# Sliding-window attention with ALiBi, then a hard-swish MLP, on one core: batches 1 and 2 transposed two pairs at a time, batch 1's diagonal without tables, loads and downs in another order

## The chip, the cores and the metric

The kernel runs on one core of one Trainium2 chip. A core has a matrix engine (TensorE, PE in the profile; its weight loads are shown as PEld), a vector engine (DVE), an activation engine (ACT), a general engine (POOL) and an engine that here only issues transfers (SP). Data lie in on-chip memory (SBUF, 128 partitions), and matmul results in eight banks of PSUM. The metric is the device time of one execution in microseconds (us), less is better. The kernel before takes 338.2 us, the median of three runs from 337.28 to 338.25.

## The reference

Inputs are q, k and v of 8 batches x 8 heads x 576 tokens x 64, in float32, and two weight matrices, 512 x 2048 and 2048 x 512.

```python
scores = scale * np.matmul(q, k.transpose(0, 1, 3, 2))
bias = slopes[:, None, None] * (-np.abs(rel).astype(np.float32))[None, :, :]
mask = (rel >= 0) & (rel < window)                 # rel = query - key, window = 128
scores = np.where(mask, scores + bias[None], -1000000000.0)
attn = softmax(scores);  out = np.matmul(attn, v)  # each head
x = out.transpose(0, 2, 1, 3).reshape(B * S, H * D)  # 4608 tokens x 512
h = x @ w_in
g = h * np.clip(h + 3.0, 0.0, 6.0) / 6.0
return g @ w_out
```

## The kernel before

**Tiling.** Two heads make a pair; pair g is batch g // 4, heads 2(g % 4) and the next. There are 32 pairs. With a window of 128, a block of 128 queries needs its own block of keys (the diagonal scores, `scores_diag`, PSUM tile `scd`) and the block before it (the off scores, `scores_off`, tile `sco`). Keys lie on the partitions and queries along the rows. The exponentials of the scores (`pd`, `po`, and for the short last block `p4buf`) are the weights of the matmuls with v (`av_matmuls`); a column of ones behind v gives the sums. The quotient `avs` is transposed into `xT`, 512 features on the partitions, which the MLP reads. The MLP takes the 4608 tokens in nine chunks of 512: 16 ups for each chunk (`moe_up`: four matmuls of 128x512 into `hps`, ACT's `r`, DVE's product into `gbuf`) and 16 downs (`moe_down`: four matmuls into `ops`; the fourth of each group of four copies `ops` out and stores 128 rows).

**Where bias and mask come from.** For batches 0 and 1 (`tabled`, `full`) a table matmul (`ident` against `tab`, lines 234, 251, 254) puts bias and mask into PSUM ahead of the scores: two of 128x512 for the diagonal of a pair, and for each head one of 128x384 and one of 128x128 for the off blocks. ACT then takes one exponential over both heads of 128x1024 (`exp_full`). For batches 2 to 7 there is no table: ACT adds the bias per partition (`bias_d`, `bias_o`) for each head, and POOL zeroes what the mask forbids (`affine_select`, lines 301, 311, 322).

**How q and k get transposed.** For batches 0 to 2 (`NB_PE`) TensorE transposes them. `load_run` brings one pair's q or k, 128 partitions x 576 float32 (288 KB, lines 91 to 95), `prepare` casts it to bf16 (line 197), and `transposes` makes 36 transposes of 64x64 for a pair (18 of q, 18 of k, line 215) into PSUM, which ACT and DVE copy into `qTb` and `kTb` (line 216). From batch 3 on, `load_tokens` brings tokens, POOL casts them into `tbuf` (line 184), and a transposing DMA from SP's queue (`xbar`, line 189) writes `qTb` and `kTb`. All loads land in four buffers, `ldbuf[0]` to `ldbuf[3]`: q of batches 0 to 2 in the first, k in the second; v0, v2 and k3 in turn in the third; v1 and q3 in the fourth.

**What sets the order.** Each engine works through its instructions in the order in which the program names them (`manual_schedule`); waits come from data and buffers alone. SP's queue is in order too: a load that waits holds what stands behind it. A transfer on the hardware queues also waits for the one eight places before it. `ps_sc` has two PSUM buffers of two banks each, used in turn by `scd`, `sco` and `attend`; `ps_h` has two of one bank for `hps`; `ps_av` and `ps_o` have one each.

**Stages.** `first_batch` does pairs 0 to 3: transposes, scores and exponentials, then values (`attend`) and the transposes into `xT` (`back`). `load_w_in` and `load_w_out` go out on POOL's queue. `second_batch` does pairs 4 to 7: scores, with ups of chunk 0 between them, then `attend` for the four pairs. `fill(n)` emits the next n units of one list of ups and downs; an up is held until `done[0]` says that all tokens of its chunk are in `xT`. `ORDER` gives the list: "U" an up of the new chunk, "D" a down of the chunk before it. `segment` does pairs 8 to 31: in round g the scores of pair g, the exponentials of g, the values of pair g - 1 (`values`, in two halves of three and two query blocks that share the one `av` bank), and `stage_next` for the next batch's casts, transposing DMAs and loads (`LOADS`, `VCAST`: the round in which a load or a cast of v is issued). Batch 1's `pd` and `po` lie in `gbuf[1]`, batch 0's in `w_out_sb`, until chunk 1 and `w_out` take the room.

The gate that starts batch 1's loads is a one-element write of POOL into `ldbuf[0]` (line 523), behind POOL's cast of the last part of v0.

Of the kernel before, what the change touches and what calls it, by code (L numbers as in the profile page):

```python
# [18 lines left out]
def kernel(  # L19
# [9 lines left out]
    nc = tc.nc  # L29
# [12 lines left out]
    NB_PE = 3  # L42
# [53 lines left out]

    def tokens(b, nm):
        if (b, nm) not in ld:
            i = 2 + b % 2 if b < 3 else (3, 2, 0, 1)[(3 * (b - 3) + "qkv".index(nm)) % 4]
            ld[b, nm] = ldbuf[i][:, 0:NQ * H * D].rearrange("p (j h d) -> p j h d", j=NQ, h=H)  # L100
        return ld[b, nm]
# [8 lines left out]
    def constants():  # L110
# [9 lines left out]
        nc.gpsimd.tensor_copy(out=base_b, in_=base_i)  # L120
        nc.gpsimd.affine_select(out=base_b[:, 1, :], in_=base_b[:, 1, :], pattern=[[1, 128]],
# [72 lines left out]
    def prepare(g, copies):  # L194
        for nm, copy in zip("qk", copies):
            pr = prs.tile([128, RT * D], BF16, tag=f"pr{nm}", name="pr")
            copy(out=pr, in_=runs[nm][:, g % NP, :])  # L197
            st[g, nm] = pr

    def transposes(g, copies, nms="qk"):  # L200
        b, hp = divmod(g, NP)
        for nm, dst, copy in (("q", qTb[b % 2], copies[0]), ("k", kTb[b % 2], copies[1])):
            if nm not in nms:
                continue
            src = st.pop((g, nm))
            pool, tag = (ps_h, "h")
            if nm == "k" and g >= NP:
                pool, tag = (ps_av, "av")
            elif NP <= g <= 2 * NP:
                pool, tag = (ps_o, "o")  # L210
            tp = pool.tile([128, RT, RP], BF16, tag=tag, name="tp", padded_shape=[128, 16, 64])
# [6 lines left out]

    def full(g):
        return g < NB_FULL * NP  # L220

    def tabled(g):
        return g < 2 * NP

    def scores_diag(g):
        b, hp = divmod(g, NP)
        qT, kT = qTb[b % 2][:, hp, :, :], kTb[b % 2][:, hp, :, :]
        first = not tabled(g)
        scd = ps_sc.tile([128, 2, 512], FP32, tag="sc", name="scd")
        st[g, "scd"] = scd  # L230
        if tabled(g):
            for e in range(2):
                t = tab[:, 2 * hp + e, 1:2, :]
                nc.tensor.matmul(scd[:, e, :].rearrange("p (j c) -> p j c", j=4), lhsT=ident,
                                 rhs=t.to_broadcast([128, 4, 128]), start=True, stop=False)
# [6 lines left out]
    def scores_off(g):  # L242
        b, hp = divmod(g, NP)
        qT, kT = qTb[b % 2][:, hp, :, :], kTb[b % 2][:, hp, :, :]
        first, foff = not tabled(g), not full(g)
        sco = ps_sc.tile([128, 2, 512], FP32, tag="sc", name="sco")
        if full(g):
# [8 lines left out]
        elif tabled(g):  # L256
            for e in range(2):
                nc.tensor.matmul(sco[:, e, 64:128], lhsT=ident,
                                 rhs=tab[:, 2 * hp + e, 1, 0:64], start=True, stop=False)
        for e in range(2):  # L260
            r = slice(e * D, (e + 1) * D)
            nc.tensor.matmul(sco[:, e, 64:128], lhsT=kT[r, 4, :],
                             rhs=qT[r, 4, 0:LAST], start=first, stop=foff)
# [6 lines left out]
        st[g, "sco"] = sco  # L270
# [13 lines left out]
    def exp_full(g):  # L284
        nc.scalar.activation(out=st[g, "pd"].rearrange("p e j c -> p e (j c)"),
                             in_=st[g, "scd"], func=ACT.Exp, scale=scale)
        nc.scalar.activation(out=st[g, "po"].rearrange("p e j c -> p e (j c)"),
                             in_=st[g, "sco"], func=ACT.Exp, scale=scale)

    def exp_diag(g, e):  # L290
        h = 2 * (g % NP) + e
        pd, sc = st[g, "pd"], st[g, "scd"]
        if tabled(g):
# [11 lines left out]
    def exp_off(g, e):  # L305
# [8 lines left out]
        if tabled(g):  # L314
            if e == 1:
                nc.scalar.activation(out=p4[:, :, 0:64], in_=sc[:, :, 64:128],
                                     func=ACT.Exp, scale=scale)
            return
# [92 lines left out]

    def moe_up(nt, ms):
        gts[nt] = gbuf[nt % 2]
        hps, n = begun.pop((nt, ms), (None, 0))
        if hps is None:
            hps = ps_h.tile([128, NT], FP32, tag="h", name="hps")
# [33 lines left out]
    ORDER = [("UUDDUDUD", "UUDDUDUD", "UUDDUDUD", "UUDDUDUD"),  # L450
# [21 lines left out]
    LOADS = {8: "k3", 9: "v3", 10: "q4", 12: "k4", 13: "v4", 14: "q5", 16: "k5", 17: "v5", 18: "q6",  # L472
             20: "k6", 21: "v6", 22: "q7", 24: "k7", 25: "v7"}

    VCAST = {12: 3, 15: 4, 19: 5, 23: 6, 27: 7}

    def stage_next(g):
        b, hp = divmod(g, NP)
        nb = b + 1
        if g == 2 * NP:  # L480
            cast_tokens(2, "v")
        if nb < B and hp < 2:
# [4 lines left out]
        for n in LOADS.get(g, "").split():  # L487
            load_tokens(int(n[1]), n[0])

    def reload(g):  # L490
        load_run(g, "q", nc.sync)
        load_run(g, "k", nc.sync)

    def first_batch():
        prepare(0, (V, A))
        warm_up(40)
# [7 lines left out]
        prepare(2, (P, P))  # L504
        transposes(2, (V, V))
# [3 lines left out]
        prepare(3, (P, V))  # L509
        transposes(3, (V, V))  # L510
# [12 lines left out]
        nc.gpsimd.memset(runs["q"][:, 0, 0:1], 0.0)  # L523
        for g in range(NP, 2 * NP):
            reload(g)
# [8 lines left out]
        prepare(NP, (P, P))  # L534
        prepare(NP + 1, (P, P))
# [3 lines left out]
        back(3)  # L539
        up_begin(0, 1, 3)  # L540
        done[0] = NP
        fill(2)
        transposes(NP, (V, A))
        biases()
        fill(1)

    def second_batch():
        for g in range(NP, 2 * NP - 1):
            scores(g)
            exp_full(g)  # L550
            fill(1)
            transposes(g + 1, (V, A))
            if g + 2 < 2 * NP:
                prepare(g + 2, (P, P))
            fill(2 if g > NP else 1)
        for j in range(NQ):
            cast_v(1, j, P)
        load_w_out(0)
        for g in range(2 * NP, 3 * NP):
            reload(g)  # L560
        load_tokens(2, "v")
        load_tokens(3, "q")
        load_w_out(1)
        prepare(2 * NP, (P, P))
        for i in range(2, 4):
# [3 lines left out]
        exp_full(g)  # L569
# [114 lines left out]
```

## Time and profile before

| What | Value |
|---|---|
| median of three runs | 338.2 us (337.28, 338.2, 338.25) |
| the profiled execution's own time | 338.87 us |
| its span, first to last instruction | 337.2 us |
| PE busy | 321.7 us (95%) |
| ACT, DVE, POOL busy | 200.2, 166.0, 137.7 us |
| mean granted TensorE clock | 0.995 |
| hardware queue q1 (loads, stores, transposing DMAs) | 41.07 MB |
| software queue q0 (`w_in`, `w_out`) | 4.19 MB |

Busy time adds up the instructions of an engine; matmuls overlap in their pipeline, so their mean duration (359 ns for 128x512) is longer than the pitch at which they follow one another (four in 0.86 us). The share of an engine is a mean over stages. The first scores stand at 7.7 us, the scores of pair 4 at 26.39, of pair 8 at 53.67, of pair 9 at 63.82, of pair 12 at 89.53 and of pair 13 at 97.95. From 319 us on only downs remain. A wait is read as the idle time of an engine just before an instruction and what ended it.

### The profile page before, as it was taken

How to read it: one execution, taken by the hardware profiler on the slowest of the kernel's cores; microseconds unless marked ns; L12 is line 12 of the kernel's file. 1: busy time of each engine (PE TensorE's matmuls, PEld its weight loads, DVE VectorE, ACT ScalarE, POOL GpSimd, SP SyncE). 2: the span in 40 equal slices, each digit the busy share in tenths (PEclk: the TensorE clock that was granted, in tenths of full speed). 3: DMA queues.
4: the chain of work that ended last, by engine and by line, in shares of the span. 5: the costliest groups of instructions: out<-in, count | busy, mean ns of one | idle time of the engine just before them, and what ended most of it. 6: DMA issues, size and time to landing. Idle time of an engine off the chain costs nothing.

```text
span 337.2 us, 7470 instructions
## 1 busy us (share of the span) xinstructions
PE 321.7 (95%) x2963; PEld 170.3 (51%) x2963; DVE 166.0 (49%) x332; ACT 200.2 (59%) x343; POOL 137.7 (41%) x243
## 2 busy tenths in 40 slices
PE   8989998998987999999999999999999999999995
PEld 7564564554443445454567665545554544444442
DVE  4656566454433645464446454554555554434410
ACT  3758875777543675767576757675676344344401
POOL 7524630866546637464746374645333000000000
PEclk9999999999997999999999999999999999999999
DMA  7999999979999899899999998993121100000111
GB/s 279 195 263 278 279 243 205 203 129 192 213 213 177 143 235 177 176 148 241 186 204 132 242 198 175 153 209 89 35 67 49 68 31 31 33 31 31 63 63 62
DMA packets 134771, 51.77 MB, mean 154 GB/s; under 512 B 122832, under 2 KB 127184, under 8 KB 134736
## 3 DMA queue, kind: packets, MB, share of 16 engines
q1 hardware_dynamic: 127200, 41.07, 62.0%
q0 software_dynamic: 4224, 4.19, 7.6%
q10 hardware_dynamic: 3312, 6.03, 5.0%
q8 instruction: 23, 0.38, 0.5%
q14 instruction: 12, 0.10, 0.1%
HBM read 36.70 MB, written 9.44 MB: 137 GB/s over the span
## 4 chain that ended last, share of the span: by engine, by line
PE 78%; ACT 5%; DMA 4%; POOL 4%; DVE 4%; issue 2%; SPq 1%; ACTq 1%; POOLq 0%
PE ops L432 33%; PE hps L403 31%; PE scd L239 3%; ACT r L419 2%; DVE gbuf L420 2%; PE tp L215 2%; DMA ldbuf<-in_k_dram 2%; PE av L343 2%; PE sco L268 2%; DMA ldbuf<-in_q_dram 2%; PE av L335 1%; POOL tbuf L184 1%; PE tb L384 1%; PE w L147 1%; ACT osb L444 1%
## 5 line engine op out<-in xcount | busy, mean ns | idle before, releaser
L420 DVE SCALAR_TENSOR_TENSOR gbuf<-r,hps 128x512 bf16<-128x512 f32 x144 | 98.5, 686 | 120.9 <-ACT r L419 120.8
L403 PE MATMUL hps<-xT,w_in_sb 128*128 128x512 bf16 (+1 forms) x640 | 147.1, 359 | 2.5 <-DVE gbuf L420 1.3
L419 ACT ACTIVATE r<-hps,bias 128x512 f32<-128x512 f32 x144 | 98.8, 689 | 82.5 <-PE hps L403 82.0
L432 PE MATMUL ops<-w_out_sb,gbuf 128*128 128x512 bf16 x576 | 142.9, 380 | 0.8 <-DVE osb L447 0.8
L403 PEld LDWEIGHTS <-w_in_sb 128*128 128x128 bf16 x640 | 59.0, 98 | 57.6 <-issue 5.8
L432 PEld LDWEIGHTS <-gbuf 128*128 128x128 bf16 x576 | 53.6, 98 | 59.4 <-issue 2.2
L301 POOL TENSOR_SCALAR_AFFINE_SELECT pd<-pd 128x512 bf16<-128x512 bf16 x48 | 29.8, 631 | 58.8 <-ACT pd L298 58.7
L311 POOL TENSOR_SCALAR_AFFINE_SELECT po<-po 128x512 bf16<-128x512 bf16 x48 | 30.2, 633 | 30.1 <-ACT po L308 29.5
L184 POOL CAST tbuf<-ldbuf 128x512 bf16<-128x512 f32 (+1 forms) x50 | 29.1, 611 | 14.2 <-DMA ldbuf<-in_k_dram 14.1
L298 ACT ACTIVATE pd<-scd,bias_d 128x512 bf16<-128x512 f32 x48 | 32.0, 688 | 4.4 <-POOL vbuf L177 2.3
L308 ACT ACTIVATE po<-sco,bias_o 128x512 bf16<-128x512 f32 x48 | 33.3, 694 | 0.4 <-ACT osb L444 0.4
L444 ACT COPY osb<-ops 128x512 f32<-128x512 f32 x18 | 10.6, 587 | 29.1 <-PE ops L432 29.1
L354 DVE TENSOR_TENSOR avs<-av,rc 128x384 bf16<-128x384 f32 (+1 forms) x48 | 23.6, 491 | 1.6
L343 PE MATMUL av<-vbuf,pd 128*128 128x65 bf16 x192 | 18.0, 194 | 2.9 <-POOL vbuf L177 2.5
L343 PEld LDWEIGHTS <-pd 128*128 128x128 bf16 x192 | 14.5, 97 | 10.2 <-issue 2.2
L335 PE MATMUL av<-vbuf,po 128*128 128x65 bf16 x192 | 18.3, 193 | 0.7 <-POOL po L311 0.7
L197 POOL CAST pr<-ldbuf 128x576 bf16<-128x576 f32 x20 | 13.0, 667 | 11.7 <-DMA ldbuf<-in_q_dram 9.1
L447 DVE COPY osb<-ops 128x512 f32<-128x512 f32 x17 | 11.7, 687 | 10.5 <-PE ops L432 10.4
L335 PEld LDWEIGHTS <-po 128*128 128x128 bf16 x192 | 14.4, 98 | 4.5 <-POOL po L311 1.0
L319 ACT ACTIVATE p4buf<-sco,bias_d 128x64 bf16<-128x64 f32 x48 | 15.8, 328 | 0.0
L239 PEld LDWEIGHTS <-kTb 64*128 64x128 bf16 x256 | 7.3, 94 | 13.3 <-issue 10.3
L353 DVE RECIPROCAL rc<-av 128x6 f32<-128x6 f32 (+1 forms) x48 | 8.8, 183 | 9.3 <-PE av L343 9.3
(79 smaller groups left out, 226.5 us busy)
## 6 DMA issues: line engine op xcount, KB each, us to landing
ldbuf<-in_v_dram SPq DMA_DIRECT2D x32, 256.0 KB, 5.4
ldbuf<-in_q_dram SPq DMA_DIRECT2D x20, 256.0 KB, 4.9
ldbuf<-in_k_dram SPq DMA_DIRECT2D x20, 256.0 KB, 4.5
out_dram<-osb ACTq DMA_DIRECT2D x18, 256.0 KB, 2.1
out_dram<-osb SPq DMA_DIRECT2D x17, 256.0 KB, 2.7
ldbuf<-in_q_dram SPq DMA_DIRECT2D x12, 288.0 KB, 6.2
ldbuf<-in_k_dram SPq DMA_DIRECT2D x8, 288.0 KB, 7.0
w_in_sb<-in_moe_w_in_dram POOLq DMA_DIRECT2D x4, 512.0 KB, 9.9
```

The source lines that it names most:

```text
L184: nc.gpsimd.tensor_copy(out=tbuf[:m, :, j, :], in_=s[:m, j, :, :].rearrange("p (i e) d -> p i (e d)", e=2))
L298: nc.scalar.activation(out=pd[:, e, :, :].rearrange("p j c -> p (j c)"), in_=sc[:, e, :], func=ACT.Exp, bias=bias_d[:, h:h + 1], scale=scale)
L301: nc.gpsimd.affine_select(out=pd[:, e, :, :], in_=pd[:, e, :, :], pattern=[[0, 4], [1, 128]], channel_multiplier=-1, base=0, compare_op=AL ...
L308: nc.scalar.activation(out=po[:, e, :, :].rearrange("p j c -> p (j c)"), in_=sc[:, e, :], func=ACT.Exp, bias=bias_o[:, h:h + 1], scale=scale)
L311: nc.gpsimd.affine_select(out=po[:, e, :, :], in_=po[:, e, :, :], pattern=[[0, 4], [-1, 128]], channel_multiplier=1, base=-1, compare_op=A ...
L335: nc.tensor.matmul(out_av, lhsT=po[:, e, qt % 4, :], rhs=vb[:, qt - 1, h, :], start=True, stop=False)
L343: nc.tensor.matmul(out_av, lhsT=d, rhs=vb[:, qt, h, :], start=(qt == 0), stop=True)
L354: nc.vector.tensor_tensor(out=st[g, "avs"][:, qts[0]:qts[0] + nq, :, :], in0=av[:, 0:nq, :, 0:D], in1=rc[:, 0:nq, :, :].to_broadcast([128, ...
L403: nc.tensor.matmul(hps[:, lo:hi], lhsT=w_in_sb[:, ks, ts(ms, 128)], rhs=xT[:, ks, ds(src, hi - lo)], start=(ks == 0), stop=(ks == n_ks - 1))
L419: nc.scalar.activation(out=r6, in_=hps, func=ACT.Relu, bias=bias3[:, 0:1], scale=1.0 / 6.0)
L420: nc.vector.scalar_tensor_tensor(out=gts[nt][:, ms, :], in0=r6, scalar=1.0, in1=hps, op0=ALU.min, op1=ALU.mult)
L432: nc.tensor.matmul(ops[nt, sub], lhsT=gts[nt][:, ms, ts(sub, 128)], rhs=w_out_sb[:, ms, :], start=(ms == 0), stop=(ms == n_ms - 1))
```

## The change

- **Loads.** `load_run` for batches 1 and 2 gives way to `load_double`: two pairs (dp 0 or 1) of q or k in two loads of 288 KB, one for the even and one for the odd heads, so that 64 runs of nine tokens of each of two pairs lie on the 128 partitions. The number and size of the loads stay; the order is k, k, q, q for two pairs, where it was q, k for each pair. The one-element write of POOL is to the q buffer still, and the first loads behind it in the program are now k's. Batch 2's loads are named in `first_batch`, behind batch 1's casts; they were named in `second_batch`, behind the casts of v1. v2 and q3 are named behind a new one-element write of POOL into `ldbuf[2]`, which stands after the casts of batch 2's first two pairs.
- **Casts.** `prepare_double`: four casts of 128x576 on POOL for two pairs, as many as before. v1's five casts go from POOL to DVE. The casts of v3 move from `stage_next` of round 12 into round 12 ahead of the values of pair 11.
- **Transposes.** Nine of 128x128 for q or k of two pairs, where there were 36 of 64x64: in batch 1 as one block in a `ps_sc` buffer (`wide_double`, one copy of 128x1152), in batch 2 as five and four in a bank of `av` or `h` (`double`). Batch 0 keeps its 64x64 form.
- **Batch 1's diagonal** has no table (`diag_tabled` holds for batch 0 alone): ACT takes two exponentials with bias, and POOL two selects on `pd`, for each pair. The off blocks keep their tables and one exponential, which now stands behind the next up's `r`.
- **Pair 0's tables** stand among the warm-up matmuls (30, where there were 40); the off tables of pairs 1 and 2 stand ahead of the next pair's transposes. `biases` moves to the start, ahead of the tables on DVE.
- **Ups and downs.** Five ups of chunk 0 use the `av` and `o` banks (`UP_BANKS`). Batch 1's `attend` calls stand among chunk 0's last four ups with one up between them; the scores of pair 8 come after the first two ups of chunk 1. Chunk 1's order in `ORDER` changes. `load_w_out` is named in one row of four. k3 and the other loads in `stage_next` come before the casts and the transposing DMA; k3 moves from `LOADS` of round 8 to the place right behind the casts of v2.

```diff
+    def load_double(b, dp, nm, eng):
+        for e in range(2):
+            eng.dma_start(out=ldbuf["qk".index(nm)][:, ds((2 * dp + e) * RT * D, RT * D)],
+                          in_=src_of[nm][b, ds(4 * dp, 4), :, :].rearrange(
+                              "(i e) (a t) d -> e i a (t d)", e=2, t=RT)[e])
...
+    def prepare_double(b, dp, copies):
+        for nm, copy in zip("kq", copies):
+            pr = prs.tile([128, RT, 2 * D], BF16, tag=f"pr{nm}", name="pr2")
+            for e in range(2):
+                copy(out=pr[:, :, ts(e, D)],
+                     in_=ldbuf["qk".index(nm)][:, ds((2 * dp + e) * RT * D, RT * D)].rearrange(
+                         "p (t d) -> p t d", t=RT))
+            st[b, dp, nm] = pr
...
+    def double(b, dp, nm, part, tag, copy):
+        src = st[b, dp, nm]
+        t0, t1 = ((0, 5), (5, RT))[part]
+        tp = BANKS[tag].tile([128, t1 - t0, 128], BF16, tag=tag, name="tp2",
+                             padded_shape=[128, 8, 128])
+        for t in range(t0, t1):
+            nc.tensor.transpose(tp[:, t - t0, :], src[:, t, :], ident)
...
+    def wide_double(b, dp, nm, copy):
+        src = st[b, dp, nm]
+        wide = ps_sc.tile([128, 2, 512], FP32, tag="sc", name="tp3")
...
+    UP_BANKS = {2: "av", 5: "o", 8: "av", 11: "o", 12: "av"}
...
-    ORDER = [("UUDDUDUD", "UUDDUDUD", "UUDDUDUD", "UUDDUDUD"),
+    ORDER = [("UUDUDUDUD", "UUDUDUDUD", "UUDUDUDD", "UUDDDD"),
...
         if g == 2 * NP:
             cast_tokens(2, "v")
+            load_tokens(3, "k")
+        for n in LOADS.get(g, "").split():
+            load_tokens(int(n[1]), n[0])
         if nb < B and hp < 2:
             cast_tokens(nb, "qk"[hp])
             xbar(nb, "qk"[hp])
         if VCAST.get(g):
             cast_tokens(VCAST[g], "v")
-        for n in LOADS.get(g, "").split():
-            load_tokens(int(n[1]), n[0])
...
         prepare(0, (V, A))
-        warm_up(40)
+        warm_up(20)
+        tables_diag(0)
+        tables_off(0)
+        warm_up(10)
         transposes(0, (V, A))
...
-        nc.gpsimd.memset(runs["q"][:, 0, 0:1], 0.0)
-        for g in range(NP, 2 * NP):
-            reload(g)
+        nc.gpsimd.memset(ldbuf[0][:, 0:1], 0.0)
+        for dp in range(2):
+            for nm in "kq":
+                load_double(1, dp, nm, nc.sync)
         load_tokens(1, "v")
...
         up_begin(0, 0, 3)
         back(3)
+        wide_double(1, 0, "q", V)
+        prepare_double(1, 1, (P, P))
+        for dp in range(2):
+            for nm in "kq":
+                load_double(2, dp, nm, nc.sync)
         up_begin(0, 1, 3)
         done[0] = NP
+        fill(1)
+        wide_double(1, 0, "k", A)
         fill(2)
-        transposes(NP, (V, A))
-        biases()
-        fill(1)
...
             scores(g)
-            exp_full(g)
+            exp_diag(g, 0)
+            exp_diag(g, 1)
             fill(1)
-            transposes(g + 1, (V, A))
-            if g + 2 < 2 * NP:
-                prepare(g + 2, (P, P))
-            fill(2 if g > NP else 1)
+            exp_off_full(g)
+            if g < NP + 2:
+                nm, eng = (("k", V), ("q", V))[g - NP]
+                wide_double(1, 1, nm, eng)
+            fill(2)
         for j in range(NQ):
-            cast_v(1, j, P)
+            cast_v(1, j, V)
...
+        prepare_double(2, 0, (P, P))
+        nc.gpsimd.memset(ldbuf[2][:, 0:1], 0.0)
+        load_tokens(2, "v")
+        load_tokens(3, "q")
+        prepare_double(2, 1, (P, P))
+        fill(1)
+        exp_off_full(g)
         attend(NP)
...
             if g < hi:
                 exp_diag(g, 1)
-            if g + 2 < NB_PE * NP:
-                prepare(g + 2, (P, P))
+            if g == 3 * NP:
+                cast_tokens(3, "v")
             if g > lo:
                 values(g - 1, (0, 1, 2))
```

## The prediction

> **What bounds the kernel now.** The page comes first: busy shares, the granted clock, the chain that ended last.
>
> ```profile
> PE 321.7 (95%) x2963; PEld 170.3 (51%) x2963; DVE 166.0 (49%) x332; ACT 200.2 (59%) x343; POOL 137.7 (41%) x243
> PE 78%; ACT 5%; DMA 4%; POOL 4%; DVE 4%; issue 2%; SPq 1%; ACTq 1%; POOLq 0%
> ```
>
> TensorE is the bound, and a microsecond is won only where TensorE loses an instruction or a wait. The table by stage (stretch, its length, then busy us of PE, PEld, DVE, ACT, POOL, then clock, DMA share, GB/s) says where it idles; I cut where the scores of pair 4, pair 8 with two ups, pair 13 and pair 14 begin or end:
>
> ```profile
> 0.00:26.39 26.39, 22.83 (x420) 16.35 (x421) 15.40 (x36) 14.74 (x19) 13.94 (x32) 1.00 1.05 248
> 26.39:55.85 29.46, 28.02 (x411) 15.52 (x409) 17.90 (x45) 21.90 (x31) 12.46 (x19) 1.00 1.12 253
> 55.85:97.95 42.10, 39.63 (x403) 20.02 (x404) 20.17 (x39) 27.82 (x52) 23.48 (x41) 1.00 1.04 188
> 97.95:110.25 12.30, 9.77 (x69) 4.50 (x69) 4.06 (x9) 6.16 (x11) 9.07 (x17) 0.86 0.95 196
> 110.25:337.20 226.95, 221.47 (x1664) 113.91 (x1663) 108.51 (x205) 129.62 (x231) 78.73 (x137) 1.00 0.60 121
> ```
>
> The last stretch has the same instructions in both kernels: from the scores of pair 13 on the list of ups and downs stands at the same place. Everything is decided before 110. The fourth stretch shows the worst place, a clock of 0.86. The timelines of PE and then POOL show it (start, us, instructions, [idle before, releaser]):
>
> ```profile
> 18.67 0.45 PE L384 MATMUL tb<-ident,avs 128*128 128x128 bf16 x5
> 24.18 0.97 PE L215 MATMUL tp<-ident,pr 64*64 64x64 bf16 x36
> 26.39 0.59 PE L234 MATMUL scd<-tab,ident 128*128 128x512 bf16 x2
> 83.14 0.20 PE L343 MATMUL av<-vbuf,pd 128*128 128x65 bf16 x1 [0.38 <-POOL pd L301]
> 102.33 0.22 PE L343 MATMUL av<-vbuf,pd 128*128 128x65 bf16 x2 [1.92 <-POOL vbuf L177]
> 103.31 0.21 PE L343 MATMUL av<-vbuf,pd 128*128 128x65 bf16 x1 [0.61 <-POOL vbuf L177]
> ```
>
> ```profile
> 22.44 0.66 POOL L197 CAST pr<-ldbuf 128x576 bf16<-128x576 f32 x1 [4.45 <-DMA ldbuf<-in_q_dram]
> 23.95 0.67 POOL L197 CAST pr<-ldbuf 128x576 bf16<-128x576 f32 x1 [0.85 <-DMA ldbuf<-in_k_dram]
> ...
> 98.46 2.83 POOL L184 CAST tbuf<-ldbuf 128x512 bf16<-128x512 f32 x5
> 101.24 2.02 POOL L177 CAST vbuf<-ldbuf 128x1024 bf16<-128x1024 f32 x2
> ```
>
> Batch 3's v is cast behind the five casts of q4, and pair 12's values wait 1.92 and 0.61 us for it. The clock pays too, as the table cut by the microsecond shows (0.50 stands before the DMA share):
>
> ```profile
> 103.00:104.00 1.00, 0.69 (x5) 0.41 (x5) 0.29 (x2) 0.00 (x0) 1.00 (x3) 0.50 1.14 214
> ```
>
> **The change, part by part.** The profiled run took 338.87 us, 1.7 around its span of 337.2; the median of the runs shown is 338.2, 0.7 lower. All sums start at 338.87.
>
> *Head (0 to 22.7).* Tables of pair 0 now stand among the warm-ups, biases before the tables on DVE. 20 warm-ups at 0.11 (40 took 4.45), 2,048 table columns at that pace (1.7) and 10 more end near 6.4 instead of 5.81; pair 0 then sheds its 0.55 of off-diagonal tables. DVE's 16 one-column operations (1.15) sit in its 1.73 idle. I book 0 (-0.5 to +0.6): the next wait covers it.
>
> *Entry into batch 1.* Before, q4 and k4 land at 22.3 and 23.8, are cast by 24.62, and scores of pair 4 start at 26.39. Now four loads (k twice, q twice, 288 KB each) feed the first transposes, and q is asked for first on PE, with all ups behind it. In slots of before the fourth lands at 27.7. But the k loads no longer stand behind the one-element memset on POOL (16.46), so SP issues them at 12.5, right behind v0; the row by microsecond has this queue empty from 14.5 to 19.5. So q takes the first two slots: 22.3 and 23.8 as latest, cast by 24.6. As k already streams when q is issued, the 2.9 us from issue to first byte (16.6 to 19.5) may be hidden; the earliest is about 22.1, cast by 22.9. From the start of q's transposes to the scores of pair 4 it takes: 9 transposes 0.52; three matmuls that begin up 1 and the one that ends up 0, 0.87; ACT's r for up 0, 0.7 with its handing over; then, queued behind it on ACT, the copy of k, 1,152 elements at 0.83 ns each (0.64 for 576 and 0.37 for 256 give that), 1.12 and 0.14 more; 3.35 in all. So these scores start at 28.05 (from 24.65) at the latest, at 26.2 (from 22.9) at the earliest. I take 27.5, nearer to the latest, since the row has the 2.9: **+1.1** (-0.2 to +1.65). w_in's first quarter now shares the engines with k (95 packets per us each, as from 20 to 30, for 195 alone) and lands near 20.8, not 18.0; up 0 asks at 21.3.
>
> *Batch 1 and its values (26.39 to 55.85).* Removed: eight 128x512 tables, 0.53 per pair, and 0.09 less per diagonal, x4 = 2.5. Transposes: four blocks of 36 at 0.70 (pairs 5 to 8) go, 2.8; two nines and two halves of batch 2 come, 36 x 0.058 (0.29 for 5 at 18.67) = 2.1. So work falls 3.2. But waits come: one PSUM pair now turns between scores and transposes. Pair 4: the transposes wait for both diagonal exps (ACT: two r 1.16, two exps 1.16 after the scores: 0.4). Pair 6: its scores wait for DVE's 1,152-element copy (0.75 at 576, so 1.35) behind an up's 0.66: 0.65. Values of pair 4 wait for v1, now five casts of 0.42 on DVE behind the last up's product, where POOL had them ready at 40: 1.2; behind them on DVE stands the product of up 12. Batch 2's halves pass the one "av" bank on, each waiting for the copy of the last (0.6 to 0.75): 1.05 in all.  With 0.1 at pair 5 that is 3.4 of waits where 1.44 was idle: -3.2 + 3.4 - 1.44 = **-1.25** (-3.2 if idle stays 1.44; +0.5 if each wait is 1.5 times as long). ACT does not bind: 3 x 0.58 + 2 x 0.58 + 0.92 = 3.8 per pair under PE's 3.8 to 4.3. On POOL eight selects (0.62) come and v1's five casts go; w_out's four loads, now in a row behind the selects of pair 6, are issued at 40.2 to 43.2 (before 40.0 to 43.4), the last landing by 59.5 for a down near 61.
>
> *Pairs 8 to 10.* Transposes before: 6 x 0.40 = 2.4; now 18 x 0.058 = 1.0. **-1.4** (-1.0 to -1.5). Their casts are on POOL by 50.
>
> [...] The row has 36 at 0.70 and 18 whole ones at 1.04 for two pairs. [...]
>
> *k3 ahead of q3's transposing DMA.* POOL's k3 casts crept from 76.4 to 81.9 behind landings; the selects of pair 10 came late and PE idled 0.38, 0.38 and 0.35 at 82.5. Now k3 goes out when v2 is cast (66), lands by 75, and the casts start when that DMA has read the buffer (75), ending at 78; selects by 80.3, PE asks at 81.2. v3 is issued before k3's transposing DMA, which then starts near 79 (before 81.94, needed 89). **-1.1** (0 to -1.2).
>
> *v3 cast ahead of the values of pair 11.* Needed one pair later; q4's casts stand behind it now. The waits 2.53 go, and the half-clock stretch: four ups' matmuls 1.71 against 0.86, four downs' 1.28 against 0.86, 1.3. **-3.85** (-2.0 to -3.9). Late next: selects of pair 12, whose po exps now follow an osb copy; they end 3.1 us after that down, needed after 4.5.
>
> *Order of ups and downs.* Two more units are spent before pair 12, whose values now have one down, not three, between their halves: **+0.1** (0 to 0.5). The 0.78 wait for the output bank (90) stays, one pair earlier.
>
> Sum: 1.1 - 1.25 - 1.4 - 1.1 - 3.85 + 0.1 = -6.4, **332.5 us**. I do not subtract the 0.7 by which the profiled run stands above the median.
>
> The clock, in this case's row: granted 0.50 from 102.7 to 106.1 after gaps of 1.92 and 0.61. The new wait before q's transposes is 0.2 to 1.9 us long; a like drop there costs at most the same 1.3. [...]
>
> **The rivals.**
> 1. Half clock at the entry (q late, gap near 1.9): 332.5 + 1.3 = 333.8. For: the row above. Against: gaps of 0.73 and 0.26 at 51 left the clock at 1.00.
> 2. Batch 1 gives nothing: its removed work turns into waits (+0.5 in place of -1.25): 334.2. For: three engines pass one PSUM pair round. Against: ACT 21.9 of 29.46.
> 3. The k loads do not come early and q's second half takes the fourth slot, 27.7: cast by 28.45, scores at 31.85, +5.45 in place of +1.1, and half clock 1.3: 338.1, no change. Against: nothing on SP but v0 stands before them.
> 4. **Slower**: v2 goes out only after a memset behind the casts of batch 2's first half, near 47.4 in place of 39.9. If it lands 7.5 later than 61.8, its casts end at 71.9, pair 8's values wait from 66.2: 5.7 and half clock 1.3: 339.5. It decides once v2 lands after 68.7. Against: from 46 to 56 v2 and w_out share packet by packet (1,557 to 1,555); starting later, w_out runs alone first, is done by 56, and v2 has the queue: about 61.8 again. Slack is 0.4 us.
> 5. The wait at pair 12 comes back by half on another cause (selects, k3): 334.4.
>
> **How the numbers follow.** A time within about 0.3% (1 us) can't be told from no change. Chances: forecast 0.42, rival 1 0.14, 2 0.17, 3 0.06, 4 0.11, 5 0.10. Faster: forecast and 1, 2, 5, 0.83; same: most of 3, 0.06; slower: 0.11. The range runs from 330.0 (batch 1 at -3.2 gives 330.6, the 0.7 below it 329.9) to 337.0, between rival 5 with rival 2 (336.2) and rival 3; above lie rivals 3 and 4.
>
> **What would show it.** Right: no idle on PE at pair 12's first values and clock 1.00 there; POOL's v3 casts ahead of its po selects; k3's casts in one piece; q's cast done before 24.7; scores of pair 4 by 28, pair 8 with two ups done by 56. Wrong: q's second load landing after 25, PE idle over 2 us before the values of pair 4, or pair 8's values waiting for v2.

## The result and the profile after

The changed kernel takes 413.28 us (median of four runs, 412.14 to 415.25), the kernel before 338.23 (337.28 to 338.42): ratio 1.223, 95% interval 1.218 to 1.229. 332.5 was forecast, so the forecast is wrong by 81 us, and in sign. The profiled run took 412.14, its span is 410.4.

The page of the changed kernel: busy us by engine, the granted clock and the DMA share in 40 slices, the chain that ended last. Below it the DMA row of the kernel before.

```profile
PE 325.9 (79%) x2690; PEld 172.8 (42%) x2729; DVE 171.3 (42%) x336; ACT 200.3 (49%) x344; POOL 140.1 (34%) x247
PEclk9975578698576999999999999999999999999999
DMA  8961112494112699999997997996911130101012
PE 59%; DMA 21%; SPq 10%; ACT 3%; issue 2%; POOL 2%; DVE 1%; ACTq 1%; DVEq 0%
```

```profile
DMA  7999999979999899899999998993121100000111
```

TensorE runs fewer instructions than before (2729 weight loads for 2963; of the matmuls that go with them the trace holds 2690) and is busy longer, 325.9 us for 321.7, because 68.3 of the first 146 us pass at a granted clock of 0.50 (mean 0.77 from 0 to 146). But the loss is idle time: 84.5 us of the span, where 15.5 stood before. Two things have entered the chain of waits, DMA with 21% (4% before) and SP's queue with 10%; and in the three slices from 31 to 62 us, where the loads of q and k run almost alone, the DMA engines show a busy share of one tenth (0.13 from 30.78 to 61.56). TensorE's list of waits (in all, times, longest) says for what:

```profile
PE tp L248 <- POOL pr L223: 37.4, 3, 27.8
PE tp L236 <- POOL ldbuf L615: 14.2, 1, 14.2
PE tp L236 <- POOL pr L223: 9.1, 2, 5.5
PE sco L304 <- ACT p4buf L358: 5.3, 1, 5.3
```

Lines 248 and 236 are the new 128x128 transposes of batches 1 and 2; the first three rows, 60.7 us, are waits for q and k (the second names the memset that stands on POOL behind the casts of q). POOL's timeline shows when the four loads for the first of these transposes landed (each cast starts as its load lands), SP's how long it took to issue the two of q:

```profile
26.52 0.66 POOL L223 CAST pr<-ldbuf 128x576 bf16<-128x576 f32 x1 [8.35 <-DMA ldbuf<-in_k_dram]
37.83 0.67 POOL L223 CAST pr<-ldbuf 128x576 bf16<-128x576 f32 x1 [10.64 <-DMA ldbuf<-in_k_dram]
44.42 0.67 POOL L223 CAST pr<-ldbuf 128x576 bf16<-128x576 f32 x1 [5.92 <-DMA ldbuf<-in_q_dram]
50.23 0.67 POOL L223 CAST pr<-ldbuf 128x576 bf16<-128x576 f32 x1 [5.14 <-DMA ldbuf<-in_q_dram]
```

```profile
16.77 17.28 SPq L98 DMA_DIRECT2D ldbuf<-in_q_dram  x2
```

The prediction had q here between 22.1 and 23.8; its second half came at 50.2. Alone a load of 288 KB took 5.8 us here (casts at 44.42 and 50.23), beside the loads of w_in 11.3 (26.52 and 37.83); before, eight such loads landed between 22.3 and 33.2, one every 1.6 us, while w_in shared the engines (from 20 to 30, 951 packets on their queue and 952 on that of w_in). SP itself is held while it issues q (the two loads of k ahead of them, of the same shape, went out in 1.25 us), so what stands behind them in its order (the next k and q, then v) is issued late too, the next k from 34.10 on. The table by stage, in a stretch where a load runs alone (length, busy us of five engines, clock, then DMA share and GB/s):

```profile
60.00:65.00 5.00, 2.31 (x15) 1.26 (x16) 1.87 (x2) 1.01 (x2) 0.67 (x1) 0.87 0.13 50
```

A share of 0.13 is 2.1 of 16 engines. The source of such a load, as the changed kernel writes it, runs over 2 heads that lie two apart, in each over 64 rows of 2,304 bytes; the kernel before took two neighbouring heads, whose rows merge into one dimension of 128. Bytes and row length are the same, and on these I had priced it. The outermost dimension of 2 and the 2.1 engines are alike; whether the one sets the other, the experiments test.

### The profile page after: what moved, and what is told of

It reads as the page before. It is cut to its first block, busy times and chain, and to the rows that moved or that the text cites. A ratio compares the mean times of both kernels' runs of the same rounds, so it can differ in the third digit from the quotient of the medians.

```text
span 410.4 us, 6984 instructions
## 1 busy us (share of the span) xinstructions
PE 325.9 (79%) x2690; PEld 172.8 (42%) x2729; DVE 171.3 (42%) x336; ACT 200.3 (49%) x344; POOL 140.1 (34%) x247
## 4 chain that ended last, share of the span: by engine, by line
PE 59%; DMA 21%; SPq 10%; ACT 3%; issue 2%; POOL 2%; DVE 1%; ACTq 1%; DVEq 0%
PE ops L474 28%; PE hps L442 24%; DMA ldbuf<-in_q_dram 12%; SPq L98 9%; DMA ldbuf<-in_k_dram 7%; DMA ldbuf<-in_v_dram 3%; PE scd L278 2%; PE av L382 1%; PE av L374 1%; ACT r L461 1%; PE sco L310 1%; DVE gbuf L462 1%; SPq L112 1%; ACT osb L486 1%; ACTq L487 1%
## 5 line engine op out<-in xcount | busy, mean ns | idle before, releaser
L442 PE MATMUL hps<-xT,w_in_sb 128*128 128x512 bf16 (+1 forms) x620 | 151.9, 371 | 3.2 <-DVE gbuf L462 0.9
L474 PE MATMUL ops<-w_out_sb,gbuf 128*128 128x512 bf16 x557 | 140.1, 381 | 2.8 <-issue 1.6
L442 PEld LDWEIGHTS <-w_in_sb 128*128 128x128 bf16 x640 | 60.9, 101 | 59.3 <-issue 9.5
L223 POOL CAST pr<-ldbuf 128x576 bf16<-128x576 f32 x16 | 10.8, 678 | 97.4 <-DMA ldbuf<-in_q_dram 50.0
L248 PE MATMUL tp<-ident,pr 128*128 128x128 bf16 x36 | 4.1, 288 | 37.4 <-POOL pr L223 37.4
L236 PE MATMUL tp<-ident,pr 128*128 128x128 bf16 x36 | 4.9, 289 | 23.3 <-POOL ldbuf L615 14.2
L248 PEld LDWEIGHTS <-pr 128*128 128x128 bf16 x36 | 3.3, 132 | 39.1 <-POOL pr L223 38.6
L250 DVE COPY qTb<-tp 128x1152 bf16<-128x1152 bf16 x2 | 2.7, 1358 | 33.9 <-PE tp L248 33.9
## 6 DMA issues: line engine op xcount, KB each, us to landing
w_in_sb<-in_moe_w_in_dram POOLq DMA_DIRECT2D x4, 512.0 KB, 15.8
```

The source lines that it names most:

```text
L442: nc.tensor.matmul(hps[:, lo:hi], lhsT=w_in_sb[:, ks, ts(ms, 128)], rhs=xT[:, ks, ds(src, hi - lo)], start=(ks == 0), stop=(ks == n_ks - 1))
L474: nc.tensor.matmul(ops[nt, sub], lhsT=gts[nt][:, ms, ts(sub, 128)], rhs=w_out_sb[:, ms, :], start=(ms == 0), stop=(ms == n_ms - 1))
```

## The experiments

**First set: is it the loads' shape?** Theory A: the outermost dimension of 2 leaves a load two DMA engines. Theory B: the loads are gated and queued badly. Theory C: the new schedule of batch 1 costs it.

*e1_load64* keeps everything and turns the two-pair load's loops inside out (64 rows outside, two neighbouring heads inside; still two loads of 288 KB for each of q and k of two pairs):

```
-        for e in range(2):
-            eng.dma_start(out=ldbuf[..][:, ds((2 * dp + e) * RT * D, RT * D)],
-                          in_=src_of[nm][b, ds(4 * dp, 4), :, :].rearrange(
-                              "(i e) (a t) d -> e i a (t d)", e=2, t=RT)[e])
+        for i in range(2):
+            eng.dma_start(out=ldbuf[..][ts(i, 64), ds(2 * dp * RT * D, 2 * RT * D)].rearrange(
+                              "a (e c) -> a e c", e=2),
+                          in_=src_of[nm][b, ds(4 * dp + 2 * i, 2), :, :].rearrange(
+                              "e (a t) d -> a e (t d)", t=RT))
```

> The changed kernel with one edit: each two-pair load (same 16 loads of 288 KB, same destinations, same places in the queue, descriptors still 2,304 B) walks 64 rows outside and two heads inside, where the changed kernel walks 2 heads outside and 64 rows inside. Theory A (a load whose outermost dimension is 2 is served by 2 of the 16 DMA engines): the casts of q and k end their waits near 20 to 24 us instead of 26.5 to 50, the scores of pair 4 start at 26.2 to 28.1 instead of 56.8, and the time is that of the sum on record without its wrong step, 332.5 us (330 to 337). Theory B (the loads come late because of what gates them: the one-element memsets on POOL, the queue's order): the casts still wait, about 413. Theory C (the new schedule of batch 1, three engines passing PSUM banks on, is what costs): loads early, but PE still waits tens of us, 390 to 413.

Measured: 338.68 us (twelve runs, 337.85 to 339.33), ratio to the kernel before 1.000 (0.997 to 1.003). So one edit of the loads takes back 75 us, with the same gates, places in the queue and schedule: B and C are out as the main cause. But A's number is missed too: it is 338.7, not 332.5. With the loads in this shape the change is worth nothing, and that is a second error, taken up in the second set.

*e2_no_gates* takes the two memsets away:

```
-        nc.gpsimd.memset(ldbuf[0][:, 0:1], 0.0)
...
-        nc.gpsimd.memset(ldbuf[2][:, 0:1], 0.0)
```

> The changed kernel without its two one-element POOL memsets of the load buffers, which hold back the q loads of batch 1 and v of batch 2; the loads themselves unchanged, so q is waited for by the real readers alone. Theory A: the loads take as long as before (5.8 us each alone, about 11 beside w_in), 408 to 414. Theory B: the gates were the cause, 330 to 350. Theory C: 408 to 414.

Measured: 410.65 us (one run). The casts of the first four loads start at 26.0, 37.3, 44.2 and 50.1, within 0.6 us of where they did with the gates. The gates are out as a cause.

*e3_before_two_rows* is the kernel before, with the shape alone:

```
-        load_run(g, "q", nc.sync)
-        load_run(g, "k", nc.sync)
+        b, hp = divmod(g, NP)
+        for nm in "qk":
+            nc.sync.dma_start(out=runs[nm][:, hp, :],
+                              in_=src_of[nm][b, ds(4 * (hp // 2), 4), :, :].rearrange(
+                                  "(i e) (p t) d -> e i p (t d)", e=2, t=RT)[hp % 2])
```

> The kernel before, with nothing changed but the source of the 16 one-pair loads of q and k of batches 1 and 2: each takes two heads that lie two apart (outermost dimension 2, then 64 rows of 2,304 B) where it took two neighbouring heads (one dimension of 128 rows). So pairs of heads are mixed differently in these two batches, and their share of the output is not the reference's; bytes, descriptors and schedule are the same. Theory A: each load takes 5 to 6 us alone, 11 beside w_in, instead of 1.4; the pairs of batch 1 need two each, the eighth lands near 74 instead of 33, and batch 2's eight come at the same pace: 375 to 415 us. Theories B and C, by which the pattern is indifferent: 337 to 340.

Measured: 417.91 us (one run), a little above the range. The old schedule with the new loads is as slow as the change. Its POOL timeline has the loads 5.9 us apart, and its table by stage the same share:

```profile
44.13 0.67 POOL L197 CAST pr<-ldbuf 128x576 bf16<-128x576 f32 x1 [5.21 <-DMA ldbuf<-in_q_dram]
50.04 0.67 POOL L197 CAST pr<-ldbuf 128x576 bf16<-128x576 f32 x1 [5.24 <-DMA ldbuf<-in_k_dram]
```

```profile
60.00:65.00 5.00, 2.27 (x22) 1.29 (x24) 0.00 (x0) 0.64 (x1) 0.67 (x1) 0.72 0.14 51
```

*e4_four_rows* is the changed kernel with four blocks of 32 rows where it had two of 64:

```
-                          in_=src_of[nm][b, ds(4 * dp, 4), :, :].rearrange(
-                              "(i e) (a t) d -> e i a (t d)", e=2, t=RT)[e])
+                          in_=src_of[nm][b, ds(4 * dp, 4), ds(e * 288, 288), :].rearrange(
+                              "i (a t) d -> i a (t d)", t=RT))
```

> The changed kernel with loads whose outermost dimension is 4 (half a head of each of four heads, 4 blocks of 32 rows of 2,304 B) where it was 2; bytes, descriptors, number and order of loads the same. Rows of different heads are exchanged in batches 1 and 2, so their share of the output is not the reference's. Theory A with the pace in proportion to the outermost dimension: each load takes 2.9 us alone and about 5.5 beside w_in, DMA share about 0.25 where it was 0.13; the fourth lands near 31 instead of 50, scores of pair 4 near 35, 338 to 352 us. A theory by which any broken-up pattern is slow, whatever its count: about 400 to 413.

Measured: 368.38 us (one run). The dose works: with 4 outside, a load alone takes 2.9 us, half of 5.8, as POOL's casts show, and the share doubles (first while the load runs alone, then beside w_in):

```profile
46.35 0.67 POOL L223 CAST pr<-ldbuf 128x576 bf16<-128x576 f32 x1 [2.42 <-DMA ldbuf<-in_k_dram]
49.29 0.67 POOL L223 CAST pr<-ldbuf 128x576 bf16<-128x576 f32 x1 [2.27 <-DMA ldbuf<-in_q_dram]
```

```profile
46.00:49.00 3.00, 2.95 (x32) 1.44 (x32) 1.38 (x2) 2.22 (x5) 0.67 (x1) 0.88 0.26 98
35.00:40.00 5.00, 0.00 (x0) 0.00 (x0) 0.00 (x0) 0.00 (x0) 0.05 (x1) 0.50 0.28 76
```

The time lies above the range that I gave (338 to 352): the fourth load landed at 40.0, not 31, since w_in was on its way until then (its last quarter landed at 40.9; the share from 35 to 40 is 0.28, where the load alone has 0.26) and each load took 5.7 to 6.3.

**Second set: where did the 6.4 us of the sum go?** The stages of the profiled runs, cut as in the prediction (entry: until the scores of pair 4 begin; batch 1: until pair 8's scores and two ups are done; then the starts of pairs 13 and 14). Differences to before, in us:

| stage | before | sum on record | change | e1_load64 |
|---|---|---|---|---|
| head and entry | 26.39 | +1.1 | +30.4 (56.82) | +7.85 (34.24) |
| batch 1 and its values | 29.46 | -1.25 | +33.2 (to 119.48) | +0.1 (to 63.79) |
| pairs 8 to 12 | 42.10 | -2.5 (-1.4 - 1.1) | +14.3 (to 175.92) | -2.7 (to 103.15) |
| pair 13 | 12.30 | -3.75 (-3.85 + 0.1) | -4.0 (to 184.27) | -4.0 (to 111.49) |
| pair 14 to the end | 226.95 | 0 | -0.8 | -0.8 |
| span | 337.2 | -6.4 | +73.2 | +0.4 |

In e1_load64 the later terms come out about as forecast, and the entry eats them. POOL's and then TensorE's timeline of it, and the table by stage (0.50 is the clock):

```profile
21.55 1.27 POOL L224 CAST pr<-ldbuf 128x576 bf16<-128x576 f32 x2 [2.13 <-DMA ldbuf<-in_k_dram]
27.32 1.28 POOL L224 CAST pr<-ldbuf 128x576 bf16<-128x576 f32 x2 [4.50 <-DMA ldbuf<-in_q_dram]
```

```profile
28.66 1.14 PE L249 MATMUL tp<-ident,pr 128*128 128x128 bf16 x9 [5.07 <-POOL pr L224]
```

```profile
32.00:33.00 1.00, 1.00 (x7) 0.56 (x5) 0.69 (x1) 0.73 (x2) 0.00 (x0) 0.50 1.23 225
```

k, issued at 12.3, took the first two places, and q the third and fourth: 27.2, where the fourth load of before landed at 27.6. For q that is rival 3 of the prediction, priced there at 338.1 and given 6 in 100. Issuing k 4.3 us earlier than the first load of before brought the first load 3.7 us ahead (18.6 for 22.3), the second 2.4 and the fourth only 0.4, since v0 and w_in fill the engines meanwhile (share 1.1 to 1.3 in each microsecond from 15 to 33). Nor did q go out earlier: v0's last part landed at 17.3 (15.6 before, 15.8 in the changed kernel), so the memset behind its cast came at 17.89 (16.46) and q's loads at 18.01, where the first of before went out at 16.59. TensorE waits 5.07 us, and after about 3.5 us of that the clock falls to 0.50, until 33.9. Theory D: this is what cost the 6 us, and the other terms hold. Theory E: they were worth little.

*e5_single_entry* gives pairs 4 and 5 their one-pair loads and 64x64 transposes back:

```
-        for dp in range(2):
-            for nm in "kq":
-                load_double(1, dp, nm, nc.sync)
+        for g in (NP, NP + 1):
+            for nm in "kq":
+                load_run(g, nm, nc.sync)
+        for nm in "kq":
+            load_double(1, 1, nm, nc.sync)
...
-        prepare_double(1, 0, (P, P))
+        prepare(NP, (P, P))
+        prepare(NP + 1, (P, P))
```

(and `transposes` of pair 4 ahead of the scores of pair 4, of pair 5 in pair 4's round.)

> The kernel of e1_load64 with pairs 4 and 5 alone put back to one-pair loads and 36 transposes of 64x64 each, in the banks of the kernel before; pairs 6 and 7 and batch 2 stay in two-pair loads. Theory D (the first transposes of batch 1 now ask for four loads, and the fourth lands at 27.2 as the fourth did at 27.7 before; the other terms of the sum on record hold): the scores of pair 4 start near 26.4 instead of 34.2 (-7.85), four blocks of 64x64 at 0.70 come for two of 9 at 0.52 (+1.8): 338.7 - 7.85 + 1.8 = 332.6, range 331 to 335. Theory E (the other terms were worth little, and the late entry is absorbed behind work that waits anyway): 337 to 340.

Measured: 335.97 us (six runs), ratio 0.991 (0.988 to 0.994). The entry is repaired, pair 4 starts at 27.1; but half of the gain is lost within one round, where k of pairs 6 and 7 is asked for before it is there:

```profile
33.23 1.14 PE L250 MATMUL tp<-ident,pr 128*128 128x128 bf16 x9 [2.93 <-POOL pr L225]
```

In this profile the clock falls at 32.7 and pair 5 starts 9.9 us after pair 4, where 4.3 were needed before. The profiled run is one of three with a mean granted clock of 0.990 to 0.995, which took 336.6 to 337.9 us; the other three, at 0.999 or 1.0, took 335.2 to 335.3. Neither D (331 to 335) nor E (337 to 340) is met by the median.

*e6_v1_on_pool* moves five casts on top of e1_load64:

```
+            if g == NP + 1:
+                for j in range(NQ):
+                    cast_v(1, j, P)
             fill(2)
-        for j in range(NQ):
-            cast_v(1, j, V)
```

> The kernel of e1_load64 with the five casts of batch 1's v on POOL after the selects of pair 5, instead of on DVE behind the last product of pair 6's round; nothing else. Theory D: the waits of TensorE for these casts (0.43, 0.49, 0.52 and 0.52 us) and the 0.67 us product behind them go, 336.7 (336.0 to 337.5). Theory E: the selects of pair 6 and the issues of w_out come later by what POOL now does, and nothing is won: 338.2 to 339.

Measured: 336.10 us (four runs), ratio 0.990 (0.987 to 0.993), as D has it. On DVE these casts had taken 3.56 us for five (0.42 for the first, 0.85 to 0.88 for each of the others; I had 0.42 for all, the shortest row), and the values of pair 4 waited four times. Two of these waits, in e1_load64:

```profile
50.87 0.19 PE L383 MATMUL wide<-vbuf,gbuf 128*128 128x65 bf16 x1 [0.43 <-DVE vbuf L178]
51.63 0.19 PE L383 MATMUL wide<-vbuf,gbuf 128*128 128x65 bf16 x1 [0.49 <-DVE vbuf L178]
```

On POOL they are gone, and batch 1 takes 27.1 us (34.15 to 61.25), 2.4 less than before.

*e7_single_entry_v1_on_pool* does both.

> Both edits together: pairs 4 and 5 by one-pair loads, the casts of v of batch 1 on POOL. Theory D: the two add, 332.6 - 2.0 = 330.6 (329.5 to 333.5), faster than the kernel before. Theory E: 337 to 340.

Measured: 335.01 us (six runs), ratio 0.988 (0.985 to 0.991). Neither D nor E is met: the two edits do not add. In its profile the values of pair 10 wait for selects (0.27, 0.38, 0.35) and the scores of pair 12 wait 1.37 us for the transposing DMA of k of batch 3, which on SP's queue now stands behind five loads of v3.

*e8_before_v3_early* is one part of the change alone, in the kernel before:

```
-    VCAST = {12: 3, 15: 4, ...}
+    VCAST = {15: 4, ...}
...
                 exp_diag(g, 1)
+            if g == 3 * NP:
+                cast_tokens(3, "v")
```

> The kernel before with one part of the change alone: the cast of v of batch 3 ahead of the values of pair 11, on POOL after the exps of pair 12's diagonal, instead of behind the five casts of q of batch 4. By the term on record: the waits of 1.92 and 0.61 us and the half clock behind them (1.3) go, -3.85 (-2.0 to -3.9): 335 us (334.9 to 336.9 where the kernel before takes 338.8). Rival: the wait comes back by half on the selects of pair 12 or on v3 itself, 336.9; or whole, 338.8.

Measured: 339.54 us (ten runs, 337.36 to 342.54), ratio 1.002 (0.999 to 1.005): nothing. Yet in its profile the stage does what I booked: no wait at pair 12's values, clock 1.00, pair 14 at 106.48 for 110.25, 3.8 us ahead. TensorE's timeline shows where most of it is given back (2.2 us by the end of the span), and SP's timeline why (each time this kernel first, then the kernel before):

```profile
133.83 0.59 PE L403 MATMUL hps<-xT,w_in_sb 128*128 128x512 bf16 x2 [2.75 <-DMA xT<-avs]
```

```profile
134.26 1.09 PE L403 MATMUL hps<-xT,w_in_sb 128*128 128x512 bf16 x4
```

```profile
123.90 5.12 SPq L107 DMA_DIRECT2D ldbuf<-in_q_dram  x5
129.12 1.40 SPq L377 DMA_TRANSPOSE xT<-avs  x1
```

```profile
123.85 5.12 SPq L107 DMA_DIRECT2D ldbuf<-in_q_dram  x5
129.07 1.40 SPq L377 DMA_TRANSPOSE xT<-avs  x1
```

The transposing DMA that brings attention rows to the ups stands behind five loads on SP's queue, and that queue goes out at the same microsecond as before. It was in time for the old TensorE, which did not wait here; for one that is 3.8 us earlier it is 2.75 late. The profiled run is the fastest of the ten. The nine others ran at a mean granted clock of 0.987 to 0.995, the profiled one at 1.0, so by these means each of them spent some 3 to 9 us at half clock, an estimate; where, and whether after this gap, is not shown (the last section has the falls in two profiles).

*e9_all_edits* adds to e7_single_entry_v1_on_pool:

```
-            if g < NP + 2:
-                nm, eng = (("k", V), ("q", V))[g - NP]
-                wide_double(1, 1, nm, eng)
+            if g == NP + 1:
+                wide_double(1, 1, "k", V)
...
+            if g == NP + 1:
+                wide_double(1, 1, "q", A)
...
(stage_next: the loads of v3 behind the transposing DMA of k3)
```

> The kernel of e7_single_entry_v1_on_pool with two more edits: both transposes of pairs 6 and 7 stand in pair 5's round (k after its diagonal exps, q two thirds through), where k's stood in pair 4's round and TensorE waited 0.74 us (2.93 in e5_single_entry) for the k loads; and the loads of v of batch 3 go to the queue behind the transposing DMA of k of batch 3, not ahead of it. Theory D (each wait in the timeline on TensorE is worth its length): 335.0 - 0.7 to 2.9 - the 1.37 us that pair 12's scores waited for that DMA, + up to 1 for the copy of q ahead of pair 6's scores: 333.0 (331.5 to 334.0). Rival F (what is left is held by a queue that does not move, as in e8_before_v3_early): 334.5 to 335.5, with a new wait on TensorE after 100 us.

Measured: 335.58 us (six runs, 333.79 to 337.45), ratio 0.990 (0.985 to 0.995). Rival F holds in kind, 0.1 us above its range: the two edits win nothing on e7_single_entry_v1_on_pool (335.01). The runs spread over 3.7 us at granted clocks of 0.993 to 1.0, which no profile here explains. In the profiled one (336.39 us) batch 1 runs from 26.69 to 55.3 with no wait over 0.51, and then TensorE meets the next late transfers, w_out (0.66 and 1.53 us) and, after 100 us, k of batch 4:

```profile
63.72 1.02 PE L476 MATMUL ops<-w_out_sb,gbuf 128*128 128x512 bf16 x4 [1.53 <-DMA w_out_sb<-in_moe_w_out_dram]
125.10 0.40 PE L280 MATMUL scd<-qTb,kTb 64*128 64x128 bf16 x8 [1.72 <-DMA kTb<-tbuf]
```

*e10_before_stage_next* is e8_before_v3_early with the change's order of loads:

```
-    LOADS = {8: "k3", 9: "v3", ...}
+    LOADS = {9: "v3", ...}
...
             cast_tokens(2, "v")
+            load_tokens(3, "k")
+        if g != 9:
+            for n in LOADS.get(g, "").split():
+                load_tokens(int(n[1]), n[0])
         if nb < B and hp < 2:
             cast_tokens(nb, "qk"[hp])
             xbar(nb, "qk"[hp])
+        if g == 9:
+            load_tokens(3, "v")
         if VCAST.get(g):
             cast_tokens(VCAST[g], "v")
-        for n in LOADS.get(g, "").split():
-            load_tokens(int(n[1]), n[0])
```

> The kernel of e8_before_v3_early with the loads of each round put ahead of its transposing DMA as in the changed kernel (except v of batch 3, which stays behind), and k of batch 3 asked for right after the cast of v of batch 2. In e8 TensorE was 3.8 us ahead at pair 14 (106.5 instead of 110.3), and lost 2.75 of it at 131, where the transposed attention rows of xT stood on SP's queue behind five loads of q of batch 5 (issued from 123.9, as in the kernel before). Theory G (the loads' place in SP's queue takes the gain back): this wait and the 0.6 us one of the kernel before go, 339 - 3.8 - 0.8 = 334.4 (333.5 to 335.5) beside 339 for the kernel before. Rival H (the gain is lost for another reason that the profile of e8 does not show, since its ten runs spread over 5 us): 337 to 340.

Measured: 333.02 us (six runs, 332.24 to 334.59), ratio 0.983 (0.980 to 0.987). It is the fastest kernel here, 1.7% faster than the kernel before, with the old loads, tables and 64x64 transposes. G holds, and the time lies 0.5 us below its range. On SP's queue the same two entries now go out 3 us and more earlier, and TensorE no longer waits for them:

```profile
120.84 4.54 SPq L107 DMA_DIRECT2D ldbuf<-in_q_dram  x5
125.48 1.41 SPq L377 DMA_TRANSPOSE xT<-avs  x1
```

By stage against before: pairs 8 to 12 41.49 (-0.6), pair 13 8.12 (-4.2), the rest 226.34 (-0.6). The order of the loads without the early cast of v3 was not run.

## Why the prediction was wrong, step by step

**Entry into batch 1** is the step that failed, at two points. First the price of a load: "288 KB each" was put into "slots of before", where loads land 1.3 to 2.5 us apart, because bytes and row length agreed. The loads' loop order was there to read: in the diff, `"(i e) (a t) d -> e i a (t d)"` puts a dimension of 2 outside. Measured: 5.8 us a load alone, 11.3 beside w_in (e1, e3 and e4 show the cause). Between e1_load64 and the changed kernel, which differ in this shape alone, lie 22.6 us at the entry, 33.1 in batch 1 and 17.1 in pairs 8 to 12. No rival named it, since all five priced the loads alike.

Second, "the k loads no longer stand behind the one-element memset", from which followed "q takes the first two slots". With the loads' shape repaired (e1_load64) k came first and q took places three and four, +7.85 in place of +1.1. An issue 4.3 us earlier was hardly an earlier landing for the load that was waited for (0.4 us), since the bytes of v0 and w_in had to pass too; and k's bytes delayed v0 and with it q's own issue. Rival 3 had q's place right, and 6.75 for the entry with its half clock against 7.85; its other condition, that k does not come early, did not hold. What was held against it, "nothing on SP but v0 stands before them", looked at the queue instead of the bytes: from 15 to 19, where the prediction read this queue as empty, the engines of the kernel before have a share of 1.20 to 1.28. Before, the first transposes needed two loads; now they needed four.

**Batch 1 and its values**, -1.25: with repaired loads +0.1. The casts of v1 on DVE were the missized term, four waits of 0.43 to 0.52 (1.96) and a product of 0.67 behind them, 1.2 booked; without them the stage is -2.4 (e6).

**Pairs 8 to 10** and **k3 ahead of q3's transposing DMA**, -2.5 together: -2.7 in e1_load64. Right in sum; in e10_before_stage_next, where k3's part (-1.1) stands without the transposes, the stage gives -0.6, so the split between the two is not shown.

**v3 cast ahead of the values of pair 11**, -3.85: right in its place in every kernel that has it (-3.8 to -4.2, clock 1.00). But I called it a term of its own, and alone it is worth nothing in the median of ten runs (e8): under "late next" I named POOL's selects and not SP's queue. Where it paid (e10), the loads' order had changed with it, which I had priced for k3 alone.

**Order of ups and downs**, +0.1, and the last stretch, 0: the stretch from pair 14 on was 0.8 us shorter than before, not equal; a wait of 0.63 us for xT, at 168.85 in the kernel before, is gone in the changed kernel, and in e1_load64 too.

**The clock**: rival 1's fall at the entry came, longer than priced (27 to 33.9 in e1_load64, 1.3 booked), with a wait of 5.07 instead of up to 1.9. And "after gaps of 1.92 and 0.61" was misread: the microsecond from 102 has a clock of 0.82, so the fall came at 102.64, after the first gap and before the second began (102.70).

## What to carry to other kernels

Price a DMA by the shape of its access pattern as well as by its bytes: the same 288 KB in rows of the same length landed every 1.6 us with 128 rows outermost (while other loads shared the engines), and took 2.9 with four and 5.8 with two, alone. Here a busy share of 0.13 to 0.14 in the table by stage, while TensorE waited for a load, showed it. Where the DMA engines are full (here a share of 1.1 to 1.3), count the bytes that must pass before the one that is waited for: here an issue 4.3 us earlier moved the fourth load by 0.4. And when a stall is removed from an engine, look up which transfer the engine asks for next and whether its queue goes out earlier too: v3's cast alone won 3.8 us at pair 13 and nothing in the whole, while the cast and the loads' order together won 1.7%.

## What the runs showed of the hardware

- In the changed kernel the slow loads also held the queue that issues them: SP needed 17.28 us to issue the two of q (16.77 to 34.05), where the two of the same size in e1_load64 took 1.5 (18.01 to 19.52), and the next k went out at 34.10. The two of k ahead of them, of the same shape, took 1.25 us, and were still under way when q was held (their casts start at 26.52 and 37.83); what limits it is not shown.
- The granted clock fell to 0.50 after idle times of different length: some 3 us after TensorE stopped at 23.2 in the changed kernel (the microsecond from 26 has 0.56), 3.5 in e1_load64, but 2.4 in e5_single_entry (30.3 to 32.7), while a gap of 2.75 in e8_before_v3_early left it at 1.00 (the mean of that run too). So the length of a gap alone does not decide it. In the kernel before the clock stood at 0.50 for 3.41 us (102.64 to 106.05), in the changed kernel seven times, for 3.41 (from 63.67, 97.80 and 142.17), 6.83 (from 73.91 and 125.11), 13.65 (from 104.63) and 30.72 us (from 26.12), each time 3.41 or a whole number of times that. In the 3.41 us ahead of a fall PE was busy for 0 to 1.34 in the changed kernel and for 1.49 in the kernel before. With both profiles cut every 3.41 us, counted from the first fall, each other stretch at 1.00 that lies whole in the span has 1.51 or more (the least from 405.00 in the changed kernel) and was followed by 1.00. The gap of e8_before_v3_early, cut at 132.37, leaves 2.13 us of work in the 3.41 ahead of the cut and 1.90 in those behind it. What decides beyond these cases is not shown. The kernel before, then the second of these two (the first time in each line is the stretch's length, the second that of PE):

```profile
99.23:102.64 3.41, 1.49 (x13) 0.70 (x12) 0.92 (x2) 1.84 (x3) 3.41 (x6) 1.00 0.42 144
132.37:135.78 3.41, 1.90 (x23) 0.98 (x24) 0.60 (x1) 0.69 (x1) 1.16 (x2) 1.00 0.66 202
```

- Casts of 128x512 from fp32 on DVE ran from 0.42 to 0.88 us in one kernel (e1_load64). Of the five of v1, all beside work on POOL, the first took 0.42 and the others 0.85 to 0.88; POOL's casts of 128x576 beside them took 0.85 to 0.86, where they take 0.67 elsewhere. What decides this is not shown.
